# A conformer layer on one core: last keys of four heads in one bank, a VectorE exponential one instruction shorter, half outputs issued beside half scores, and a reordered end

## Chip, cores and metric

The kernel runs on one core of one Trainium2 chip. The metric is the device time of one execution in microseconds (us). The kernel before takes 991.62 us (median of 3 runs, 990.72 to 992.05).

Names used below: PE is TensorE's matrix multiply, PEld its weight load, DVE is VectorE, ACT is ScalarE, POOL is GpSimd. In the views, PT holds exponentials, PS is any bank of PSUM, OTF the attention outputs copied out for their transposes, XN rows normalised by POOL, U the gated input of the convolution, TH a tanh, and HT the hidden layer of a feed-forward.

## The reference

Two sequences of T = 4000 tokens, D = 144 features, H = 4 heads of 36. A feed-forward (half residual), attention, a gated convolution over 5 tokens, a second feed-forward, a layer norm. What matters here is attention, with 2 x 4 x 4000 x 4000 = 128 million exponentials, and the convolution, which couples each token to two neighbours on either side:

```python
scores = jnp.einsum('bhqd,bhkd->bhqk', q, k) * scale
p = _softmax(scores, axis=-1)
att = jnp.einsum('bhqk,bhkd->bhqd', p, v)
...
pad = K // 2                                   # K = 5
hp = jnp.pad(h, ((0, 0), (pad, pad), (0, 0)))
for i in range(K):
    c = c + hp[:, i:i + T, :] * dw[i][None, None, :]
x = x + _silu(c) @ w_pw2
h = _layernorm(x, axis=-1)
h = _silu(h @ w_ff2a) @ w_ff2b
x = x + 0.5 * h
return _layernorm(x, axis=-1)
```

## The kernel before

The program is written by a planner. It keeps an estimated clock for each engine, picks the next piece of work by it, and records instructions. What comes out is a fixed order for each engine with semaphore waits between them; nothing is decided on the chip. So any change of a cost or a rule gives a whole new order.

Queries come in 16 chunks of 500 tokens, keys in 63 tiles of 64 (4000 = 62 x 64 + 32, so the last tile is half padding): 16 x 63 = 1008 tiles. A tile serves 4 heads: in two banks of PSUM, partitions 0 to 63 and 64 to 127 hold two heads each, so one tile is 4 score multiplies of 64 x 64 (one per quadrant of the array), 1000 exponentials on 128 partitions, and 4 output multiplies.

```python
def scores(n, hh, bk, cost):           # half a tile: two heads, one bank, array rows 64*hh
    for p in range(2):
        op("pe", "matmul", PSV[64*p:64*p+64, bk, 0:CH],
           lhsT=KT[64*hh:64*hh+64, p, b, k0:k0+KT_ROWS], rhs=QT[64*hh:64*hh+64, p, q0:q0+CH], ...)

def emit_S(n):                         # a tile for ACT: both halves, all four quadrants
    lo, hi = banks.take_pair()
    scores(n, 0, lo, 0.0525)
    scores(n, 1, hi, 0.0525)

def emit_exp(n, lo, hi):
    op("act", "activation", PT[:, pt, :, :], PSV[:, lo:hi+1, 0:CH], ACT.Exp, scale=ATT_SCALE, ...)

def emit_O(m):                         # outputs of one tile: array rows 64*p
    for hh in range(2):
        for p in range(2):
            op("pe", "matmul", PSV[64*hh:64*hh+DH+1, BX+p, 0:CH],
               lhsT=VA[64*p:64*p+64, blk, hh, 0:DH+1], rhs=PT[64*p:64*p+64, pt, hh, :], ...)
```

Some tiles have their exponential computed on DVE instead, with bit operations and a polynomial. For these the two halves of the scores are issued one at a time, each in its own bank:

```python
def dve_tile(n):
    for hh in range(2):
        bk = yield need("pe", banks, dur=0.21, kind="q")
        scores(n, hh, bk, 0.105)
        ...
        op("dve", "tensor_scalar", PTU[:, z, hh, :], PSV[:, bk, 0:CH], ATT_SCALE*LOG2E*256.0, 127.5*256.0, ...)
    op("dve", "tensor_scalar", mm, zz, 0xFF, 0x6400, op0=bitwise_and, op1=bitwise_or)        # mantissa as f16
    op("dve", "tensor_scalar", zz, zz, 1, 0x7F80, op0=logical_shift_right, op1=bitwise_and)  # exponent
    op("dve", "tensor_scalar", mf, mf, 1.0/256, v - 4.5, op0=mult, op1=add)
    op("dve", "tensor_tensor", mf, mf, mf, op=mult)
    op("dve", "tensor_scalar", mf, mf, E2B, 1.0 - E2B*v*v, op0=mult, op1=add)
    op("dve", "tensor_tensor", PT[:, z], PT[:, z], mf, op=mult)

def due():                             # give the next tile to DVE?
    ...
    return (... and R.free["dve"] < R.free["pe"] + DSLACK and R.free["pe"] > last_dve[0] + DGAP)
```

The end of a chunk (normalising its outputs through transposes, W_o, gate) is `epilogue` and `post1`; convolution, second feed-forward and store are `post2`, which waits for the next chunk's gate because of the two tokens on the right:

```python
def post2(c):
    z = yield need("pe", swp, cond=lambda: c in glu_done and (last or c + 1 in glu_done))
```

The softmax here doesn't subtract the row's maximum and nothing guards it: scores larger than these inputs give would overflow.

Of the kernel before, what the change touches and what calls it, by code (L numbers as in the profile page):

```python
# [12 lines left out]
D = 144  # L13
# [10 lines left out]
CH = 500  # L24
KT_ROWS = 64
# [4 lines left out]
E2A, E2B = 0.7029418, 0.23986403  # L30
# [287 lines left out]
def bass_standalone__conformer_family_zipformer__speech_kernel(  # L318
# [19 lines left out]
    NT = (T + KT_ROWS - 1) // KT_ROWS  # L338
    TP = NT * KT_ROWS

# [25 lines left out]
    BMIN = 1.5  # L366
    DRAIN = 0.6
    LATE = 0.3
    FIRST = 0.3
    DGAP = 4.0  # L370
# [10 lines left out]
    XT = sb("XT", [NXT, 2, CH])  # L381
    XTQ = sb("XTQ", [2, TP])
    TH = sb("TH", [NTH, CH])
    HT = sb("HT", [NHT, 4, CH])
    HT5 = sb("HT5", [NHT, 2 * TB])
    QT = sb("QT", [2, N])
    KT = sb("KT", [2, Bsz, TP])
    VA = sb("VA", [Bsz * NT, 2, 40])
# [6 lines left out]
    SW1 = sb("SW1", [NSW, CH])  # L395
    SW2 = sb("SW2", [NSW, TB])
# [66 lines left out]
    op("pool", "memset", NHALF[:, :], -0.5, w=["NHALF"])  # L463
    op("act", "activation", DUM[:, :], NHALF[:, 0:1], ACT.Silu, bias=0.0, scale=1.0, r=["NHALF"], w=["DUM"], cost=1.6)
# [10 lines left out]
    op("dve", "memset", KT[:, :, :, T:TP], 0.0, w=["KTZ"])  # L475
    op("dve", "memset", XTQ[:, :, T:TP], 0.0, w=["XTQZ"])
    op("dve", "memset", VA[:, :, :, DH:DH + 1], 1.0, w=["VA1a"], cost=0.5)
    tail_rows = T - (NT - 1) * KT_ROWS
    if tail_rows < KT_ROWS:
        for half in range(2):  # L480
            for b in range(Bsz):
                r0 = 64 * half + tail_rows
                op("dve", "memset", VA[r0:64 * half + 64, b * NT + NT - 1, :, DH:DH + 1], 0.0, r=["VA1a"],
                   w=["VA1"], cost=0.2)
# [30 lines left out]
    def copy(dst, src, r, w, n, rate=1.0):  # L515
        if flex() == "act":
            op("act", "activation", dst, src, ACT.Copy, bias=0.0, scale=1.0, r=r, w=w, cost=c_act(n))
        else:
            op("dve", "tensor_copy", dst, src, r=r, w=w, cost=c_dve(n, rate))

    def setup_dw():
# [18 lines left out]
        for i in range(KCONV):  # L540
            op("dve", "tensor_scalar", DG[:, i, :], IDENT[:, :], DWT[:, 0, i:i + 1], None, op0=ALU.mult,
               r=["DWT", "ID"], w=["DG"], cost=0.2)
        for o in range(3):
# [16 lines left out]
    def transp(src, rk, dst, wk, n):  # L560
        bk = yield need("pe", banks, dur=0.11 * n)
        ps = PSH[0:HD, bk, 0:256 * n].rearrange("p (k i n) -> p k i n", k=2, i=n)
        for k in range(2):
            for i in range(n):
                op("pe", "transpose", ps[:, k, i, 0:TB], src[:, i, k * HD:(k + 1) * HD], IDENT[0:TB, 0:TB],
                   r=[rk, "ID"], w=[("ps", bk)], cost=0.055, kind="f")
        yield need("dve", hold=True)
        copy(dst.rearrange("p k (i n) -> p k i n", i=n), ps[:, :, :, 0:TB], [("ps", bk)], wk, 2 * n * TB, 2.0)
        banks.give(bk)

    def ln(c, bs):
        n, b0 = len(bs), bs[0]
        u = yield need("dve", xnp)
        for j in range(n):
            op("dve", "bn_stats", ST[0:TB, u, j, :], X[0:TB, c * NB + b0 + j, :], r=[("X", c, b0 + j)],
               w=[("ST", u, j)], cost=0.21)
        yield need("dve")
        for j in range(n):
            op("dve", "bn_aggr", MV[0:TB, u, j, :], ST[0:TB, u, j, :], r=[("ST", u, j)], w=[("MV", u)], cost=0.08)
        calm = mode["front"] or mode["tail"]  # L580
# [8 lines left out]
        if not calm:  # L589
            op("pool", "tensor_scalar", RS[0:TB, u, 2, 0:n], MV[0:TB, u, 0:n, 0], -1.0, None, op0=ALU.mult,  # L590
               r=[("MV", u)], w=[("NM", u)], cost=0.3)
            for j in range(n):
                op("pool", "tensor_scalar", XN[0:TB, u, j, :], X[0:TB, c * NB + b0 + j, :], RS[0:TB, u, 2, j:j + 1],
                   RS[0:TB, u, 0, j:j + 1], op0=ALU.add, op1=ALU.mult,
                   r=[("X", c, b0 + j), ("NM", u), ("RS", u)], w=[("XN", u)], cost=XN_COST)
        else:
            yield need("dve")
            for j in range(n):
# [5 lines left out]
    XN_COST = 0.5  # L604
    POW_COST = 1.1

    def ln_tr(c, s, bs):
        u = yield from ln(c, bs)
        yield from transp(XN[0:TB, u, 0:len(bs), :], ("XN", u), XT[0:HD, s, :, bs[0] * TB:(bs[-1] + 1) * TB],
                          [("XT", s, i) for i in bs], len(bs))  # L610
        xnp.give(u)
# [11 lines left out]
    def residual(c, g, mm, scale, rk):  # L623
# [3 lines left out]
        for i in range(2):  # L627
# [8 lines left out]
           cost=c_dve(2 * D))  # L636
        banks.give(bk)

    def mm2(W0, s, m0, m1, bk, rows, wk):
        for k in range(2):  # L640
            op("pe", "matmul", PSV[0:rows, bk, 0:CH], lhsT=W0[0:HD, k, m0:m1], rhs=XT[0:HD, s, k, :], start=k == 0,
# [7 lines left out]
    def ff_tile(s, h, m, WA, WE, nm, silu):  # L649
# [4 lines left out]
        if m < 4:  # L654
            mm2(WA, s, m * 128, m * 128 + 128, bk, 128, [(nm, "a", 0)])
            n, dst = CH, HT[:, h, m, :]
        else:
            for k in range(2):
                for g in range(2):
                    op("pe", "matmul", PSV[:, bk, 0:2 * TB], lhsT=WE[0:HD, k, 64 - 64 * g:192 - 64 * g],  # L660
                       rhs=XT[0:HD, s, k, g * 2 * TB:(g + 1) * 2 * TB], start=k == 0 and g == 0, stop=k == 1 and g == 1,
                       r=[("XT", s, 2 * g), ("XT", s, 2 * g + 1), (nm, "a", 1), (nm, "a", 2), (nm, "a", 3)], w=[("ps", bk)], cost=c_pe(2 * TB),
                       kind="f")
            n, dst = 2 * TB, HT5[:, h, :]
# [13 lines left out]
    def ff(c, s, WA, WE, WB, nm, silu, then):  # L678
        h = yield need("pe", htp)
        kids = S.spawn(ff_tile(s, h, m, WA, WE, nm, silu) for m in range(5))  # L680
# [6 lines left out]
        def terms(i):  # L687
            return [(HT[:, h, m, i * TB:(i + 1) * TB], WB[:, m, :]) for m in range(4)] + [
                (HT5[:, h, (i % 2) * TB:(i % 2 + 1) * TB], WB[:, 4 + i // 2, :])]

        def half(g):
            yield from residual(c, g, terms, 0.5 if silu else 0.25, [("HT", h)] + [(nm, "b", j) for j in range(5)])
# [15 lines left out]
    def proj(dst, Wt, nm, c, p):  # L708
# [8 lines left out]
        copy(dst, PSV[:, bk, 0:CH], [("ps", bk)], [(nm + "T", c)] + [("SAVE", i) for i in range(NQ) if over], CH)  # L717
        banks.give(bk)
# [3 lines left out]

    def vproj(c, t0, t1):
# [3 lines left out]
        rk = ["WQKV", "XTQZ"] + [("XTQ", cc, i) for cc in range(CPB) for i in range(NB)  # L727
# [9 lines left out]
        copy(VA[:, b * NT + t0:b * NT + t1, :, 0:DH],  # L737
# [19 lines left out]
    def pre2(c):  # L757
# [9 lines left out]
        t0, t1 = (tiles_by(cc - 1) if cc else 0), tiles_by(cc)  # L767
        vs = []
# [57 lines left out]

    def post1(c, a):
# [20 lines left out]
        kids = S.spawn((glu(c, s2), glu_left(c, s2)))  # L848
        yield need("pool", kids=kids, cond=lambda: cc == 0 or c - 1 in glu_done)
        xtp.give(s2)  # L850
        u, up = c % NU, (c - 1) % NU
        if cc == 0:
            op("pool", "memset", U1[:, u, 2:4, 0:1], 0.0, w=[("UL", u)], cost=0.1)
            op("pool", "memset", U2[0:LP, u, 0:1], 0.0, w=[("UL", u)], cost=0.1)
        else:
            op("pool", "tensor_copy", U1[:, u, 2:4, 0:1], U1[:, up, 2:4, TB:TB + 1], r=[("U", up)], w=[("UL", u)],
               cost=0.25)
            op("pool", "tensor_copy", U1[:, up, 0:2, TB + 1:TB + 2], U1[:, u, 0:2, 1:2], r=[("U", u)],
               w=[("UR", up)], cost=0.25)
            op("pool", "tensor_copy", U2[0:LP, u, 0:1], U2[0:LP, up, TB:TB + 1], r=[("V", up)], w=[("UL", u)],  # L860
               cost=0.25)
            op("pool", "tensor_copy", U2[0:LP, up, TB + 1:TB + 2], U2[0:LP, u, 1:2], r=[("V", u)], w=[("UR", up)],
               cost=0.25)
        if cc == CPB - 1:
            op("pool", "memset", U1[:, u, 0:2, TB + 1:TB + 2], 0.0, w=[("UR", u)], cost=0.1)
            op("pool", "memset", U2[0:LP, u, TB + 1:TB + 2], 0.0, w=[("UR", u)], cost=0.1)
        glu_done.add(c)

    def conv(c, z, silu):
# [18 lines left out]
        yield from conv_act(z, bk, None if silu else t, ML, SW1[:, z, :], "SW", CH)  # L888
# [16 lines left out]
    def conv_left(c, z, silu):  # L905
# [8 lines left out]
        yield from conv_act(z, bk, None if silu else t, LP, SW2[0:LP, z, :], "SX", TB)  # L914

    def post2(c):
        cc = c % CPB
        last = cc == CPB - 1
        z = yield need("pe", swp, cond=lambda: c in glu_done and (last or c + 1 in glu_done))
# [380 lines left out]
```

## Time and profile before

| | before |
|---|---|
| time, median | 991.62 us |
| span of the profiled execution | 988.6 us |
| front, until the first exponential | 25.2 us |
| body, first to last exponential | 920.7 us |
| tail, from there to the end | 42.7 us |
| tiles on ACT / on DVE | 899 / 109 |

The busy time of the body and of the tail (columns: length, then busy us and instructions of PE, PEld, DVE, ACT, POOL; granted clock, DMA share, GB/s):

```profile
25.24:945.93 920.69, 865.75 (x10935) 369.31 (x10933) 792.07 (x2058) 900.19 (x1114) 281.42 (x487) 1.00 0.01 4
945.93:988.60 42.67, 34.23 (x441) 29.38 (x441) 25.00 (x106) 12.07 (x24) 9.12 (x18) 0.93 0.04 11
```

ACT works 900.2 of the body's 920.7 us. DVE's groups of the exponential by shape (busy us, mean ns | idle before):

```profile
L167 DVE TENSOR_TENSOR PT<-PT 128x1000 bf16<-128x1000 bf16 x109 | 74.2, 685 | 0.9
L167 DVE TENSOR_TENSOR PT<-PT 128x1000 f16<-128x1000 f16 x109 | 73.1, 678 | 0.9
```

Who is on the chain that ended last, and how long exponentials waited for scores (us, times, longest):

```profile
ACT 56%; PE 29%; DVE 11%; POOL 3%; issue 1%; POOLq 0%; DVEq 0%
```

```profile
ACT PT L167 <- PE PS L167: 13.8, 23, 1.8
```

The mean duration of a group on ACT includes overlap with its neighbours. For sums I therefore took from the trace's ACT records of the body, for each instruction, by how much its end passes the end before it ("occupied"), and the gap before it ("idle"). Before: 899 exponentials occupy 811.9 us (0.903 each), 141 tanh of 500 elements 68.6, the rest 19.7; sum 900.2 occupied, 20.5 idle.

A part of this idle time comes in single stops, which the prediction did not look at. PE waits for a tile that POOL makes, and ACT then waits for PE. One of them:

```profile
142.05 0.63 PE L167 MATMUL PS<-IDENT,XN 125*72 125x125 bf16 x8 [1.98 <-POOL XN L167]
```

```profile
142.75:146.16 3.41, 3.41 (x31) 1.22 (x24) 0.71 (x2) 2.30 (x3) 2.74 (x6) 0.50 0.00 0
```

PE stood still for 1.98 us, and 0.70 us after it goes on its granted clock falls to 0.50 for 3.41 us (third number from the end); ACT is busy for only 2.30 us of these. The body before has two such pairs (at 142 and 695 us) and one more stop of over 1 us for POOL (at 749 us). Together 5.1 of the 20.5 us of idle lie at them.

### The profile page before, as it was taken

To read this page: it belongs to the slowest core of one execution; us is meant where nothing else is said; L and a number is where in the kernel's file an instruction comes from. 1 tells how busy PE (TensorE), PEld (TensorE's weight loads), DVE (VectorE), ACT (ScalarE), POOL (GpSimd) and SP (SyncE) were. 2 spreads that over 40 slices of the span, in tenths; PEclk is the share of its full clock that TensorE was granted. 3 is DMA by queue.
4 is the path that set the end of the run, shared out by engine and by line. 5 is a ranking of instruction groups with operands and counts; after the bars stand their busy time and mean duration, and the time that the engine had idled before them with its cause. 6 is when DMAs were issued, how large, how long until landed. Compare 5 with 4: busy or idle time off the path is not lost.

```text
span 988.6 us, 27456 instructions
## 1 busy us (share of the span) xinstructions
PE 923.5 (93%) x11672; PEld 418.0 (42%) x11672; DVE 836.8 (85%) x2260; ACT 924.2 (93%) x1159; POOL 298.5 (30%) x525
## 2 busy tenths in 40 slices
PE   9999989999999999999999999999899999999997
PEld 7443424343443434444444344343344333434365
DVE  7888777999699798977879898899899997985965
ACT  4898989999999999999999999999999999999943
POOL 3221032132442225313714132235112522433212
PEclk9999999999999999999999999999999999999999
DMA  4000000000000000000000000000000000000000
GB/s 123 14 1 2 1 2 2 2 2 1 3 1 2 2 2 8 1 2 14 1 2 7 2 8 1 7 8 2 1 7 2 7 2 7 8 2 7 7 8 13
DMA packets 7422, 7.36 MB, mean 7 GB/s; under 512 B 2349, under 2 KB 7300, under 8 KB 7300
## 3 DMA queue, kind: packets, MB, share of 16 engines
q1 hardware_dynamic: 6144, 5.14, 1.8%
q8 instruction: 91, 1.49, 0.7%
q10 hardware_dynamic: 1156, 0.47, 0.2%
q14 instruction: 31, 0.25, 0.1%
HBM read 3.31 MB, written 2.30 MB: 6 GB/s over the span
## 4 chain that ended last, share of the span: by engine, by line
ACT 56%; PE 29%; DVE 11%; POOL 3%; issue 1%; POOLq 0%; DVEq 0%
ACT PT L167 50%; PE PS L167 29%; ACT TH L167 6%; DVE PT L167 5%; POOL XN L167 2%; POOL RS L167 1%; DVE ST L167 1%; DVE HT L167 1%; DVE XT L167 1%; DVE X L167 1%; DVE OTF L167 0%; DVE AN L167 0%; DVE MV L167 0%; DVE QT L167 0%; ACT HT L167 0%
## 5 line engine op out<-in xcount | busy, mean ns | idle before, releaser
L167 ACT ACTIVATE PT<-PS 128x1000 bf16<-128x1000 f32 x899 | 839.0, 1063 | 15.7 <-PE PS L167 13.8
L167 PE MATMUL PS<-QT,KT 64*64 64x500 bf16 x4032 | 419.1, 385 | 34.5 <-ACT PT L167 26.4
L167 PE MATMUL PS<-PT,VA 64*37 64x500 bf16 x4032 | 364.0, 377 | 6.4 <-ACT PT L167 2.9
L167 PEld LDWEIGHTS PS<-QT,KT 64*64 64x64 bf16 x4032 | 125.7, 104 | 236.1 <-ACT PT L167 170.2
L167 POOL TENSOR_SCALAR RS<-MV 125x4 f32<-125x4 f32 x116 | 39.0, 336 | 472.6 <-DVE MV L167 467.8
L167 DVE TENSOR_SCALAR PT<-PT 128x1000 uint16<-128x1000 uint16 (+1 forms) x436 | 177.1, 419 | 5.0
L167 PEld LDWEIGHTS PS<-PT,VA 64*37 64x37 bf16 x4032 | 115.8, 95 | 125.9 <-issue 36.8
L167 DVE TENSOR_SCALAR PT<-PS 128x500 uint16<-128x500 f32 x218 | 145.9, 670 | 16.4 <-PE PS L167 15.3
L167 POOL TENSOR_SCALAR XN<-X,RS 125x144 bf16<-125x144 bf16 x232 | 146.2, 642 | 6.0
L167 DVE TENSOR_TENSOR PT<-PT 128x1000 f16<-128x1000 f16 (+1 forms) x218 | 145.6, 681 | 1.8
L167 POOL TENSOR_TENSOR RS<-RS,NHALF 125x4 f32<-125x4 f32 (+1 forms) x102 | 99.4, 976 | 128.3 <-DVE RS L167 123.2
L167 ACT ACTIVATE TH<-PS 128x500 bf16<-128x500 f32 (+2 forms) x205 | 111.8, 570 | 3.2 <-PE PS L167 2.9
L167 DVE SCALAR_TENSOR_TENSOR HT<-TH,PS 128x500 bf16<-128x500 bf16 (+1 forms) x145 | 87.0, 616 | 27.2 <-ACT TH L167 26.3
L167 DVE SCALAR_TENSOR_TENSOR X<-PS,X 125x288 bf16<-125x288 f32 x128 | 57.1, 453 | 31.3 <-PE PS L167 29.8
L167 DVE BATCH_NORM_STATS2 ST<-X 125x6 f32<-125x144 bf16 x320 | 75.4, 295 | 2.4 <-DMA X<-in_x_dram 2.1
L167 PE MATMUL PS<-XT,WA 72*128 72x500 bf16 x256 | 72.6, 379 | 3.0 <-DVE HT L167 2.6
L167 PE MATMUL PS<-WB,HT 128*125 128x144 bf16 x640 | 61.2, 234 | 0.3
L167 PEld LDWEIGHTS PS<-WB,HT 128*125 128x125 bf16 x640 | 47.4, 137 | 26.0 <-issue 16.3
L167 PE MATMUL PS<-IDENT,XN 125*72 125x125 bf16 x512 | 42.8, 221 | 6.7 <-POOL XN L167 5.0
L167 DVE COPY XT<-PS 72x1000 bf16<-72x1000 bf16 (+1 forms) x65 | 40.2, 620 | 8.3 <-PE PS L167 7.9
L167 PEld LDWEIGHTS PS<-IDENT,XN 125*72 125x72 bf16 x512 | 31.4, 112 | 26.7 <-issue 11.4
L167 POOL COPY U<-U 128x2 bf16<-128x2 bf16 (+1 forms) x56 | 12.6, 256 | 79.2 <-DVE U L167 79.2
(78 smaller groups left out, 627.8 us busy)
## 6 DMA issues: line engine op xcount, KB each, us to landing
X<-in_x_dram SPq DMA_DIRECT2D x16, 140.6 KB
out_dram<-XN SPq DMA_DIRECT2D x13, 140.6 KB
out_dram<-XN SPq DMA_DIRECT2D x6, 70.3 KB
WA<-in_w_ff1a_dram ACTq DMA_DIRECT2D x1, 144.0 KB
WB<-in_w_ff1b_dram ACTq DMA_DIRECT2D x1, 144.0 KB, 2.7
WA<-in_w_ff2a_dram SPq DMA_DIRECT2D x1, 144.0 KB
WB<-in_w_ff2b_dram SPq DMA_DIRECT2D x1, 144.0 KB
WQKV<-in_w_qkv_dram ACTq DMA_DIRECT2D x1, 121.5 KB
```

The source lines that it names most:

```text
L167: ins = getattr(eng, o.name)(*o.a, **o.k)
```

## The change

The intent is to take exponentials off ACT, in four parts. (1) The last 32 keys: 32 keys of four heads fill 128 partitions of one bank, so the last tile of a chunk costs 500 exponentials in place of 1000. (2) DVE's chain loses one instruction: the exponent is no longer cut out; the polynomial is added to the integer form, as a mixed uint16 and f16 addition. (3) A half score of a DVE tile is issued beside half an output of another tile, on the other rows of the array. (4) At the end, chunk 15 goes first and carries the last two tokens of chunk 14, so chunk 14's convolution does not wait for it; the output copy of chunk 15 is split over DVE and ACT. `BMIN`, a limit on finished chunks whose later stages lag behind, goes from 1.5 to 2.0.

```diff
-    BMIN = 1.5
+    BMIN = 2.0
 def emit_S(n):
+    if t == NF:                                    # (1) last 32 keys: one bank
+        for p in range(2):
+            op("pe", "matmul", PSV[64*p:64*p+64, bk, 0:CH], lhsT=KL[:, b, p, :], rhs=QT[:, p, c*CH:(c+1)*CH], ...)
+        return bk, None
 def emit_exp(n, lo, hi):
+    if hi is None:
+        op("act", "activation", PT[:, pt, 0, :], PSV[:, lo, 0:CH], ACT.Exp, ...)
+        return
 def dve_tile(n):
-        scores(n, hh, bk, 0.105)
+        m = partner(1 - hh)                            # (3) an output whose input is ready
+        scores(n, hh, bk, 0.105 if m is None else 0.0525)
+        if m is not None:
+            emit_O(m, (1 - hh,))
...
-    op("dve", "tensor_scalar", zz, zz, 1, 0x7F80, op0=logical_shift_right, op1=bitwise_and)      # (2)
-    op("dve", "tensor_scalar", mf, mf, 1.0/256, v - 4.5, op0=mult, op1=add)
+    op("dve", "tensor_scalar", mf, mf, sc/256, (off - 4)*sc, op0=mult, op1=add)
     op("dve", "tensor_tensor", mf, mf, mf, op=mult)
-    op("dve", "tensor_scalar", mf, mf, E2B, 1.0 - E2B*v*v, op0=mult, op1=add)
-    op("dve", "tensor_tensor", PT[:, z], PT[:, z], mf, op=mult)
+    op("dve", "tensor_tensor", zz, zz, mf, op=add)
+    op("dve", "tensor_scalar", zz, zz, 256*(E2[0] - 1) - (off*sc)**2, 0.5, op0=add, op1=mult)
...
 def epilogue(c, part):                                # (4)
+    elif c == NCH - 1:
+        op("dve", "tensor_copy", OTF[:, 0, :], ps[:, 0, :], ...)
+        op("act", "activation", OTF[:, 1, :], ps[:, 1, :], ACT.Copy, ...)
 def post2(c):
-    cond=lambda: c in glu_done and (last or c + 1 in glu_done)
+    cond=lambda: c in glu_done and (last or c == NCH - 2 or c + 1 in glu_done)
+    e = c == NCH - 1                                   # two more columns in conv, residuals, norms
```

The cuts leave out how the two extra tokens pass through each stage, and how half-issued outputs are counted. The diff holds three more changes that are in none of the four parts: the planner now counts rows normalised by POOL as ready 0.5 us after their instruction ends, in place of 0.1 (`XN_LAT`); the convolution's border copies on POOL are planned as a thread of their own (`halo`); and the four output multiplies of a tile are issued by array rows (`for p ... for hh`) and no longer by columns.

## The prediction

> **What bounds the kernel now.** I read the page first (busy shares, slices), then the busy time by stretch, then the groups by shape, then the chain of waits, and last the timeline of the end. Three engines look full on the page:
>
> ```profile
> PE 923.5 (93%) x11672; PEld 418.0 (42%) x11672; DVE 836.8 (85%) x2260; ACT 924.2 (93%) x1159; POOL 298.5 (30%) x525
> ```
>
> A mean over the span hides which one is full where the time is spent. The table by stretch (columns: busy us and instruction count of each engine, granted clock, DMA share, GB/s) shows it:
>
> ```profile
> 0.00:25.00 25.00, 23.28 (x296) 19.25 (x298) 19.48 (x96) 11.93 (x22) 7.99 (x20) 1.00 0.45 123
> 200.00:300.00 100.00, 97.04 (x1275) 43.49 (x1274) 85.92 (x228) 99.18 (x121) 36.56 (x71) 1.00 0.01 2
> 700.00:800.00 100.00, 92.59 (x1175) 39.25 (x1175) 94.56 (x228) 98.94 (x121) 25.37 (x42) 1.00 0.02 5
> 950.00:989.00 39.00, 31.52 (x413) 26.95 (x411) 23.48 (x104) 11.81 (x23) 9.12 (x18) 0.94 0.05 13
> ```
>
> ACT (the fourth pair) is at 99% from 200 to 900 us; DVE is below it, and PE's 92 to 97% is pipelined, overlapping time. The chain of waits says the same: 50% of the span is ACT writing PT (the exponentials). So there are three parts: a front of 25 us, a body from 25.2 us to 945.9 us paced by ACT, and a tail of 42.7 us (988.6 - 945.9) in which ACT is nearly idle and one dependency chain sets the end. The change leaves the front's ACT order as it is (the first 123 ACT instructions of the two streams are the same), so I work on body and tail only.
>
> What one ACT instruction costs in the body has to be read from the chain, because the mean of a group (1063 ns) includes overlap with its neighbours:
>
> ```profile
> 924.28 14.35 ACT PT L167 x16
> 938.62 0.48 ACT TH L167
> 939.10 2.69 ACT PT L167 x3
> ...
> 945.03 0.91 ACT PT L167
> 945.93 0.04 issue
> 945.98 0.42 PE PS L167 x4
> 946.40 0.02 issue
> 946.42 1.21 DVE OTF L167
> ```
>
> 14.35/16 = 0.897 us for a full exponential (1000 elements), 0.48 us for a tanh of 500. Check of the whole body: 899 exponentials x 0.897 = 806.4; 141 tanh of 500 x 0.48 = 67.7; 27 tanh of 250 x 0.27 = 7.3; 29 small tanh x 0.17 = 4.9; copies (15 x 0.48 and two small) 7.5; sum 893.8 of 920.7 us. The other 26.9 us are ACT's idle time (20.5 by the same table over the body, over half of it before 150 us) and small gaps.
>
> The tail, in the timeline of PE:
>
> ```profile
> 945.98 0.39 PE L167 MATMUL PS<-PT,VA 64*37 64x500 bf16 x4 [0.42 <-ACT PT L167]
> 947.68 2.43 PE L167 MATMUL PS<-IDENT 128*128 128x128 bf16 x26 [1.31 <-DVE OTF L167]
> 949.91 1.16 PE L167 MATMUL PS<-IDF,OTF 128*125 128x128 f32 x4
> 950.86 1.51 PE L167 MATMUL PS<-WB,HT 128*125 128x144 bf16 x15
> 952.21 0.65 PE L167 MATMUL PS<-IDF,OTF 128*125 128x128 f32 x4
> ```
>
> The 26 filler multiplies write into the bank that the OTF copy reads, so they wait for the copy and then run in front of the transposes that need it: 2.2 us lost.
>
> **What the Trainium skill says.** "ScalarE: Activation LUTs", section "What ACT_TABLE_LOAD costs": 186 ns + 0.833 ns per element, back-to-back instructions overlapping by about 93 ns. That gives 0.926 us for 1000 and 0.51 us for 500; the trace has 0.897 and 0.48, so a half-width exponential costs 0.48, more than half of a full one. "VectorE: DVE Perf Modes", section "The perf-mode tier table": 16-bit tensor_scalar in SBUF runs 4x, tensor_tensor 2x, a PSUM source at most 2x; the trace agrees (1000 elements: 415 to 424 ns and 678 to 685 ns; 500 from PSUM 670 ns). Its section "What auto-detection actually checks" makes the mode a matter of 16-bit size, not of type, so the new uint16 + f16 addition should keep 2x; no instruction of this trace mixes the two, so it is unproven here. "TensorEngine Tiling (Array Packing)", section "Key Properties": tiles of the array work independently, and a change of tiling mode drains the engine. The trace agrees on the first: 8 quadrant multiplies last 0.61 us, 4 last 0.39, so four more cost 0.22, one full pass.
>
> **The change part by part.** The counts are of the instruction streams of the two built programs.
>
> (1) Last keys. Of 1008 key tiles (16 chunks x 63), 16 have only 32 real keys, and half the partitions of their 1000-wide exponential were padding. Now the 32 keys of all four heads share the 128 partitions of one bank: 16 exponentials of 500. PE gains nothing: two 500-column multiplies on 64 columns each in place of four quadrant ones, both about 0.21 us.
>
> (2) Shorter VectorE chain. A tile on VectorE took 2 reads from PSUM, 4 tensor_scalar and 2 tensor_tensor; by the means of their groups 2 x 670 + 4 x 420 + 2 x 681 ns = 4.38 us. Now one tensor_scalar less: 3.96 us. With that room the order gives VectorE 123 tiles in place of 109. VectorE's busy sum for this: 109 x 4.38 = 477 before, 123 x 3.96 = 487 after: 10 us more, in a shorter span: about 850/964 = 88%. The saving is spent on taking work from ACT.
>
> (3) So ACT's full exponentials go from 899 to 869. The sum for ACT's body: -30 x 0.897 = -26.9; +16 x 0.48 = +7.7; six tanh of 500 and one of 250 leave the body (a feed-forward of a late chunk now falls into the tail, partly from the higher backlog limit): -6 x 0.48 - 0.27 = -3.2. **Together -22.4 us**, body 920.7 to about 898. With 98% of ACT's time busy there, I take this one to one and leave the 26.9 us of idle and gaps unchanged.
>
> (4) Half outputs beside half scores. 204 of 246 half scores get a partner, but only 30 output tiles are split over two partners; 144 have one half riding and the other alone, which in full passes saves nothing. Saved: 30 x 0.21 = 6.3 us; the 14 more VectorE tiles cost 14 x 0.21 = 2.9, and the engine changes between kinds of work 35 times more. For PE a wash; PE is not the bound, so 0 us on the path. It makes room, no more.
>
> (5) Tail. Chunk 15 goes first and carries two tokens of chunk 14, whose convolution no longer needs chunk 15. In the stream: the OTF copy is split over DVE and ACT (1.21 to about 0.67: -0.5); four real multiplies stand where the 26 fillers stood, and don't wait for OTF (-2.2); between the two transposes stand 4 multiplies of 0.21 in place of 15 of 0.06 (-0.6); the 31 fillers before the convolution give way to 15 real multiplies (-0.8). Against it: a feed-forward of an earlier chunk, with five Silu (2.3 us) and the table load (1.28 us), now lies on ACT ahead of the copies that the chain needs (+0.7, my guess), and from the convolution to the last multiply the stream holds 17.2 us by the rates above against 15.7 (+1.5: extra two-column multiplies, two convolutions one after the other with fillers between). **Sum about -1.9 us**: tail 42.7 to 40.8. The order at the end stays: chunk 15's feed-forward, then chunk 14's, then its normalisation and store. So the dependence that is removed is only partly used.
>
> Sum: 991.6 - 22.4 - 1.9 = **967 us**, 2.5% less.
>
> **The rivals.** (a) VectorE becomes the bound. For it: it reached 94.6% in 700 to 800 us, single stretches of 10 us are above 97%. Against: in that very stretch ACT was still at 98.9%, and a tile now costs 0.4 us less. If ACT's idle grew by half its 20.5 us: 977. (b) The mixed addition falls to one element per cycle: 1000/0.96 ns in place of 500/0.96, +0.5 us x 123 = 64 us of VectorE, 95% busy; ACT would then wait often: 985 to 1000. (c) PE, its order fixed at build time, stalls where a half output is not ready when the order expects it, and the scores behind it come late: a few us, 970 to 972. (d) PE profits more than counted, because a half output alone overlaps with the next half pass on the other rows, and removes some of the 13.8 us that exponentials wait for PE: 960 to 963.
>
> **Range and chances.** ACT's count is certain; what isn't is idle time in the body (-4 to +8) and the tail (-3 to +3). That gives 960 to 975 for 8 in 10. The 2% line is at 971.8, 4.8 us above my value: 0.80 for faster by over 2%, 0.18 within, 0.02 slower, the last for (b) with more.
>
> **What would show it.** Right: the last exponential ends near 923 us, 869 full ones at 0.897 and 16 halves near 0.48, ACT at 98 to 99% from 200 us on; the mixed addition near 680 ns, no group of DVE at 1.1 us; DVE near 88%; the tail 39 to 43 us, with the transposes of OTF about 1 us after the last output. Wrong: ACT idle well above 21 us in the body (a, c), an addition at 1.1 us (b), exponentials slower than 0.897, or a tail that grows because chunk 13's leftovers delay chunk 15.

## More of the kernel before

All executions used here are fast, with a mean granted TensorE clock between 0.988 and 1.00. Time and clock go together: of the 21 executions of the kernel before that were timed beside the experiments, the eight at 0.990 took 992.05 to 992.78 us, the seven at 0.993 took 989.87 to 990.61, and the only one at 0.997 took 987.92.

## The result, and the profile after

The kernel after takes **968.89 us** (median of 4, 968.71 to 969.11) against 991.73 (median of 4) for before. The ratio is 0.9772 (95% interval 0.9755 to 0.9788). A ratio here is always the mean time of one kernel's fast runs over that of the other's of the same rounds, so not quite the ratio of the quoted medians. The profiled span is 967.1 us, 21.5 less than before. About 3 us of the difference go with the clock: the one execution of the kernel before at the clock of the kernel after, 0.997, took 987.92 us where the mean of its 21 is 991.08 (an estimate, from that single execution).

```profile
PE 911.4 (94%) x11539; PEld 411.2 (43%) x11539; DVE 849.0 (88%) x2271; ACT 907.9 (94%) x1147; POOL 295.0 (31%) x521
```

The same table for one stretch of the body, for the body and for the tail:

```profile
200.00:300.00 100.00, 96.08 (x1244) 41.89 (x1238) 91.07 (x221) 95.89 (x119) 32.98 (x60) 1.00 0.01 2
```

```profile
25.24:925.88 900.64, 854.62 (x10839) 365.73 (x10835) 797.51 (x2042) 879.92 (x1093) 276.50 (x482) 1.00 0.01 4
925.88:967.10 41.22, 33.23 (x408) 26.26 (x404) 31.48 (x134) 15.97 (x33) 10.51 (x18) 0.93 0.06 15
```

The body is 20.0 us shorter, the tail 1.5, the front is the same. ACT's busy time in the body fell by 20.3 us, its idle time did not move (20.5 and 20.7 us by my sum). In 200 to 300 us ACT is now at 95.9%, so the equal sum hides a change of place. The body after has no stretch at half clock, and one stop of PE for POOL of over 1 us (1.54 us, at 604 us) with 0.7 us of ACT's idle at it. So the stops gave back 4.4 us, and idle elsewhere grew by 4.6 (15.4 to 20.0).

ACT's and DVE's groups by shape:

```profile
L168 ACT ACTIVATE PT<-PS 128x1000 bf16<-128x1000 f32 x869 | 811.4, 1050 | 15.0 <-PE PS L168 13.5
...
L168 ACT ACTIVATE PT<-PS 128x500 bf16<-128x500 f32 x16 | 10.1, 630 | 0.1
```

```profile
L168 DVE TENSOR_TENSOR PT<-PT 128x1000 uint16<-128x1000 uint16 x123 | 83.9, 685 | 1.1
L168 DVE TENSOR_TENSOR PT<-PT 128x1000 f16<-128x1000 f16 x123 | 83.7, 683 | 1.3
```

The mixed addition (the uint16 group) takes 685 ns, as the f16 multiply beside it takes 683. The chain has changed more than the sums have:

```profile
ACT 48%; PE 35%; DVE 14%; POOL 2%; issue 1%; POOLq 0%; DVEq 0%
```

Before, 56% of the chain was ACT; now 48%, with PE and DVE taking the difference. More often than before, the piece that ended last came through a score or a DVE tile. That was the first sign that "ACT alone sets the pace" is not the whole story.

The end, in PE's timeline (start us, us, tiles, count):

```profile
926.25 0.41 PE L168 MATMUL PS<-PT,VL 64*101 64x500 bf16 x2
926.60 1.02 PE L168 MATMUL PS<-XT,WA 72*128 72x500 bf16 x4
927.45 0.68 PE L168 MATMUL PS<-IDF,OTF 128*125 128x128 f32 x4
...
928.82 0.60 PE L168 MATMUL PS<-IDF,OTF 128*125 128x128 f32 x4
```

Four real multiplies stand where the 26 fillers stood, and the transposes of OTF start 1.20 us after the last outputs start (927.45 - 926.25), where before it was 3.93 us (949.91 - 945.98). Part of that is clock: before, PE was at half clock from 948.30 to 951.71 us. Later in the tail, ACT's timeline (the value in brackets is idle time before, and who ended it):

```profile
951.06 2.31 ACT L168 ACTIVATE HT<-PS 128x502 bf16<-128x502 f32 x5 [0.69 <-PE PS L168]
...
955.35 1.54 ACT L168 ACTIVATE HT<-PS 128x500 bf16<-128x500 f32 x3 [1.53 <-PE PS L168]
```

HT of 502 columns is chunk 15's last feed-forward (500 and the two riders); HT of 500 after it is chunk 14's, which therefore ends last, with its normalisation and store behind it.

### The profile page after: what moved, and what is told of

It reads as the page before. It is cut to its first block, busy times and chain, and to the rows that moved or that the text cites. A ratio compares the mean times of both kernels' runs of the same rounds, so it can differ in the third digit from the quotient of the medians.

```text
span 967.1 us, 27192 instructions
## 1 busy us (share of the span) xinstructions
PE 911.4 (94%) x11539; PEld 411.2 (43%) x11539; DVE 849.0 (88%) x2271; ACT 907.9 (94%) x1147; POOL 295.0 (31%) x521
## 4 chain that ended last, share of the span: by engine, by line
ACT 48%; PE 35%; DVE 14%; POOL 2%; issue 1%; POOLq 0%; DVEq 0%
ACT PT L168 42%; PE PS L168 35%; DVE PT L168 8%; ACT TH L168 5%; DVE ST L168 1%; POOL XN L168 1%; DVE X L168 1%; POOL RS L168 1%; DVE HT L168 1%; DVE XT L168 1%; ACT HT L168 0%; DVE OTF L168 0%; DVE MV L168 0%; DVE XN L168 0%; DVE AN L168 0%
## 5 line engine op out<-in xcount | busy, mean ns | idle before, releaser
L168 ACT ACTIVATE PT<-PS 128x1000 bf16<-128x1000 f32 x885 | 819.3, 1043 | 15.1 <-PE PS L168 13.5
L168 PE MATMUL PS<-PT,VA 64*37 64x500 bf16 x3968 | 375.7, 376 | 7.0 <-ACT PT L168 3.8
L168 DVE TENSOR_SCALAR PT<-PS 128x500 uint16<-128x500 f32 x246 | 164.5, 670 | 19.7 <-PE PS L168 18.8
L168 DVE TENSOR_TENSOR PT<-PT 128x1000 f16<-128x1000 f16 (+1 forms) x246 | 166.9, 684 | 2.4
L168 DVE TENSOR_SCALAR PT<-PT 128x1000 uint16<-128x1000 uint16 (+1 forms) x369 | 152.0, 423 | 3.0
L168 POOL TENSOR_SCALAR XN<-X,RS 125x144 bf16<-125x144 bf16 x228 | 137.4, 615 | 5.9
L168 POOL TENSOR_TENSOR RS<-RS,NHALF 125x4 f32<-125x4 f32 (+2 forms) x103 | 98.7, 960 | 122.7 <-DVE RS L168 117.6
L168 DVE SCALAR_TENSOR_TENSOR HT<-TH,PS 128x500 bf16<-128x500 bf16 (+1 forms) x140 | 83.8, 615 | 15.9 <-ACT TH L168 15.4
L168 PE MATMUL PS<-XT,WA 72*128 72x500 bf16 (+1 forms) x256 | 72.9, 379 | 2.6 <-DVE HT L168 1.2
L168 PEld LDWEIGHTS PS<-WB,HT 128*125 128x125 bf16 x645 | 47.1, 135 | 26.2 <-issue 15.6
L168 PE MATMUL PS<-IDENT,XN 125*72 125x125 bf16 (+1 forms) x514 | 42.9, 221 | 3.9 <-POOL XN L168 2.0
L168 PEld LDWEIGHTS PS<-IDENT,XN 125*72 125x72 bf16 (+1 forms) x514 | 31.5, 112 | 24.3 <-issue 9.8
```

What stands on the lines that cost most here:

```text
L168: ins = getattr(eng, o.name)(*o.a, **o.k)
```

## The experiments

The number was close, but it rested on two claims that the profile after makes doubtful: that pairing half outputs with half scores is worth nothing on the path because PE is not the bound, and that DVE's added work lies beside ACT. Theory A in the expectations is the prediction's own account; the other letters are its rivals. Each kernel was timed against the kernel before in the same rounds; after's own ratio is 0.9772, taken in other rounds, so differences between a variant and after are differences of two ratios, times 991 us. They are not corrected for the clock. All twelve gave the reference's result.

A word on method: e1 to e8 are planned anew, so each has its own order. e9 and e10 keep after's order on every engine and add work inside it.

| run | tiles on DVE | ratio | against after, us | body, us | ACT occupied / idle, us | tail, us | of idle, at stops, us |
|---|---|---|---|---|---|---|---|
| before | 109 | 1 |  | 920.7 | 900.2 / 20.5 | 42.7 | 5.1 |
| after | 123 | 0.9772 |  | 900.6 | 879.9 / 20.7 | 41.2 | 0.7 |
| e1 | 120 | 0.9893 | +12.0 | 912.2 | 882.0 / 30.2 | 41.2 | 5.6 |
| e2 | 117 | 0.9788 | +1.6 | 904.4 | 884.9 / 19.6 | 38.7 | 0.0 |
| e3 | 109 | 0.9857 | +8.4 | 913.3 | 893.2 / 20.1 | 36.6 | 0.0 |
| e4 | 122 | 0.9817 | +4.5 | 907.1 | 886.8 / 20.3 | 37.5 | 0.7 |
| e5 | 121 | 0.9813 | +4.1 | 907.6 | 881.5 / 26.2 | 37.2 | 3.5 |
| e6 | 116 | 0.9957 | +18.3 | 917.3 | 894.1 / 23.2 | 41.1 | 3.2 |
| e7 | 116 | 0.9995 | +22.1 | 921.3 | 895.7 / 25.7 | 40.3 | 8.4 |
| e8 | 123 | 0.9849 | +7.6 | 903.2 | 878.8 / 24.3 | 49.5 | 4.3 |
| e9 | 123 | 0.9837 | +6.4 | 906.5 | 883.2 / 23.3 | 41.2 | 0.8 |
| e10 | 123 | 1.0197 | +42.1 | 941.0 | 893.9 / 47.2 | 41.9 | 4.0 |
| e11 | 131 | 0.9732 | -4.0 | 898.3 | 873.6 / 24.8 | 37.6 | 7.3 |
| e12 | 132 | 0.9730 | -4.2 | 899.2 | 874.2 / 25.0 | 35.8 | 3.0 |

The front, not in the table, varies from 24.7 to 26.9 us. The last column is ACT's idle time within 1 us before and 5.5 us after each stop of PE of over 1 us that POOL ended, and around two stretches at half clock that no such stop precedes (e8 at 55 us, e10 at 944). Of the 15 stretches at half clock in the bodies of all traces, 13 follow such a stop; seven stops of 1.03 to 1.64 us are followed by none. Where these stops fall changes with the order, so they blur every comparison of two orders.

One more measure: the score and output multiplies of the trace that start within 60 ns of each other (up to four) were counted as one pass of the array. The kernel before needs 2181 passes, after 2120, and "half-filled" below means a pass with two multiplies.

### e1_no_pair: no half output beside a half score

```diff
 def partner(p):
+    return None
```

> The changed kernel without the pairing of half outputs with half scores; all else as changed; the scheduler then gives VectorE 120 tiles in place of 123. Theory A (my prediction: ACT's count alone sets the body, PE is a wash): three exponentials more on ACT, 3 x 0.90 = +2.7 us, about 971.6 us, ACT idle in the body still near 20.7 us. Rival B (the pairing makes room on PE that the path needs): 975 us or more, with ACT idle in the body of 25 us or more, waiting for PE.

Measured 980.45 us (980.12 to 980.78), ratio 0.9893 (0.9878 to 0.9908). The body is 11.6 us longer than after's. Three more exponentials on ACT are 2.3 us of that (788.0 - 785.7 occupied; 2.1 in the sum of all ACT work); 9.5 us are ACT idle, 4.9 of them at stops for POOL. This is the line of waits for ACT, of e1:

```profile
ACT PT L168 <- PE PS L168: 23.3, 32, 2.4
```

After has 13.5 us there (its group line above). What pairing does is seen in PE's timeline. After, around 277 us:

```profile
277.41 0.40 PE L168 MATMUL PS<-QT,KT 64*64 64x500 bf16 x2
277.41 0.39 PE L168 MATMUL PS<-PT,VA 64*37 64x500 bf16 x2
```

and e1, around 309 us:

```profile
308.72 0.37 PE L168 MATMUL PS<-QT,KT 64*64 64x500 bf16 x2
308.96 0.40 PE L168 MATMUL PS<-PT,VA 64*37 64x500 bf16 x4
```

In after, two score multiplies and two output multiplies start in the same hundredth of a microsecond: one pass for both. In e1 the half score has 0.24 us to itself before the four outputs start. Over the kernel, e1 has 2177 passes, 374 of them half-filled; after has 2120 and 264. The 57 passes x 0.21 us are 12 us of PE time. That this is the size of the loss is chance: e9 below shows 0.07 us of body for each added pass, so 57 passes are some 4 us (an estimate), which fits the 4.6 us by which idle grew away from the stops. The prediction had saved only 30 passes. Theory A's 971.6 is off by 9 us for this order.

### e5_no_pair_alt: the same with another order

```diff
-    DSLACK = 0.6
+    DSLACK = 0.4
-    DGAP = 4.0
+    DGAP = 3.5
 def partner(p):
+    return None
```

> Again no pairing, but with two scheduler settings changed (least gap between VectorE tiles 3.5 in place of 4.0, slack 0.4 in place of 0.6), so that another order comes out (121 tiles). It separates the pairing from the luck of one order. Theory C (without pairing PE runs some 57 passes of 0.21 us more and ACT waits for it): 975 us or more, ACT idle in the body 26 us or more, 2165 quadrant passes or more. Rival (the +11.6 us of the first run without pairing were one unlucky order): 972 us or less.

Measured 972.25 us (970.53 to 972.82), ratio 0.9813 (0.9790 to 0.9836). Also without pairing, but 8 us faster than e1. The two expectations are split: the total is at the rival's bound, the idle at Theory C's. Body +7.0 us over after, 5.5 of it ACT idle, 2.8 of that at one stop of PE for POOL of 2.74 us; 2161 passes, 41 more than after; the tail is 4.0 us shorter. So taking pairing away costs the body 7.0 to 11.6 us in these two orders, but 2.8 to 4.9 of that are stops, which no run ties to pairing. What is left, 4.2 to 6.7 us, is idle elsewhere (2.6 and 4.6) and exponentials (1.6 and 2.1). The order alone moves the total by several us. That is the error bar of every single variant that is planned anew.

### e2_long_chain: the old six-operation chain on DVE

```diff
-        zz, zz + mf (uint16 + f16), then (zz + k) * 0.5
+        zz = (zz >> 1) & 0x7F80; mf = mf*E2B + k; PT = PT * mf        # one instruction more
```

> The changed kernel with the longer VectorE chain of before (4 tensor_scalar and 2 tensor_tensor per tile); the scheduler then takes 117 tiles. Theory A: six exponentials more on ACT, 6 x 0.90 = +5.4 us, about 974.3 us, ACT idle unchanged near 21 us, VectorE at about 90% (117 x 4.38 = 512 us of tiles against 487). Rival (VectorE becomes the bound with the long chain): above 978 us with ACT idle above 26 us.

Measured 970.09 us (969.95 to 970.21), ratio 0.9788 (0.9774 to 0.9803). The longer chain gets 117 tiles in place of 123; six exponentials more on ACT, body +3.8 us, of the size of 6 x 0.90 = 5.4 less 1.1 of idle. But the tail is 2.6 us shorter, so little is left in the total. The expectation, 974.3, was 4.2 us too slow, most of it because it held the tail constant. Its rival, DVE as the bound with the long chain, is out for this order: idle did not grow.

### e3_cap_109: everything new, but DVE gets no more tiles than before

```diff
-        if n >= NIT or not DVE_EXP or ...
+        if n >= NIT or stats["dve"] >= 0.1062 * n + 2 or not DVE_EXP or ...
```

> The changed kernel with VectorE's tiles held to 109, spread evenly, as many as before. Theory A: 14 exponentials go back to ACT, 14 x 0.90 = +12.6 us, about 981.5 us, ACT idle near 20 us. Rival (the gain comes from PE room or other waits, not from the count): below 976 us.

Measured 976.94 us (976.52 to 977.23), ratio 0.9857 (0.9843 to 0.9872). Its body:

```profile
25.24:938.50 913.26, 867.60 (x10893) 368.19 (x10891) 764.65 (x1969) 893.16 (x1113) 274.53 (x496) 1.00 0.01 4
```

The body is 12.6 us longer than after's, and 14 x 0.90 = 12.6. Idle is the same (20.1 and 20.7). This is the best test of the prediction's main term, that a tile moved from DVE to ACT costs its exponential, one to one; it is one order, planned anew, without any stop for POOL. The total lies between the two expectations, only 8.4 us slower, because the tail is 4.7 us shorter.

### e4_full_last: the last tile padded and two banks wide, as before

```diff
-    NF = T // KT_ROWS;  NT = NF + 1          # last tile apart, in one bank
+    NT = NF = (T + KT_ROWS - 1) // KT_ROWS   # with the zero padding and its memsets back
```

> The changed kernel with the last 32 keys as before: a padded 1000-wide tile in two banks in place of one bank of 500. 886 full exponentials in place of 869 full and 16 half: 17 x 0.904 - 16 x 0.498 = +7.4 us. Theory A: about 976.3 us. Rival (the one-bank form costs PE drains at the change of array mode, which this takes away): 972 to 974 us.

Measured 971.82 us (971.56 to 975.21), ratio 0.9817 (0.9795 to 0.9840). Full exponentials 886 in place of 869, no halves: 17 x 0.904 - 8.0 = +7.4 by the sum; ACT occupied +6.9 (its exponentials 800.7 against 785.7 and 8.0), body +6.5. The term holds in the body; the tail gave 3.8 back, so the total came out at the rival's 972 us. Idle did not fall (20.3), so the rival's reason, drains of PE in the body, is not seen; it is not excluded either.

### e6_pair_only and e7_short_only: one part alone

e6 is built from the kernel after, with the other three parts and `BMIN` set back; the three further changes named above and the priority of chunk 15 at the end stay in it. e7 is the kernel before with only the shorter chain.

```diff
 # e6, what differs from before, in the main (the record has its diff against after)
+        m = partner(1 - hh)
+        scores(n, hh, bk, 0.105 if m is None else 0.0525)
+        if m is not None: emit_O(m, (1 - hh,))
 # e7, against before
+        the five-operation chain in dve_tile, nothing else
```

> Pairing alone: the changed kernel with the long VectorE chain, the padded last tile, no tokens riding, no split copy and the old backlog limit. The scheduler finds 116 tiles. Theory C (PE's passes are the second bound, so pairing pays by itself): 7 exponentials off ACT, -6.3 us, and a little idle: 981 to 985 us beside 990.6. Rival (my prediction: pairing is a wash by itself, VectorE's room is what is needed): 989 us or more.

> The shorter VectorE chain alone, put into the kernel before; 116 tiles. My prediction's sum: 7 exponentials off ACT, 7 x 0.90 = -6.3 us: 984.3 us, ACT idle unchanged at 20.5 us. Theory C: more VectorE tiles mean more half-filled PE passes, so without pairing ACT's idle grows to 25 us or more and half or more of the gain is lost: 987 us or more.

e6: 985.70 us (985.43 to 987.79), ratio 0.9957 (0.9933 to 0.9980). e7: 989.62 us (988.43 to 992.12), ratio 0.9995 (0.9969 to 1.0021). Both have 892 exponentials on ACT in place of 899, so 6.3 us less by the sum. e6 keeps 3.4 of it in the body. e7 keeps none: occupied falls by 4.5 and idle rises by 5.2 (20.5 to 25.7). I read that at first as PE's extra passes (2204, 23 more than before) coming back as waits of ACT. The trace doesn't bear this out. e7 has four stops for POOL, three of them followed by 3.41 us at half clock; the longest:

```profile
144.39 0.63 PE L167 MATMUL PS<-IDENT,XN 125*72 125x125 bf16 x8 [3.14 <-POOL XN L167]
```

They hold 8.4 us of its idle, where before has 5.1: 3.3 of the 5.2. Away from the stops idle grew by 1.8 us in e7, and by 4.6 in e6, which has pairing and some 30 passes fewer than before. So these two runs don't show that passes decide. The mean clock of e7's runs (0.991) was also lower than that of the kernel before beside it (0.993). The shares of the parts don't add up: 0.4% and 0.05% alone, while undoing pairing in the whole costs 0.4 to 1.2%.

### e8_no_ride: chunk 14's two tokens wait for chunk 15 again

```diff
-        e = c == NCH - 1
+        e = False
-        cond=lambda: c in glu_done and (last or c == NCH - 2 or c + 1 in glu_done)
+        cond=lambda: c in glu_done and (last or c + 1 in glu_done)
```

> The changed kernel with chunk 14's last two tokens not riding with chunk 15 (chunk 14's convolution waits for chunk 15 again); priorities and the split copy stay; 123 tiles. My prediction gives riding little: body as in the changed kernel (900.6 us), tail 41 to 43 us: 969 to 971 us. Rival (with chunk 15's priority the dependence holds chunk 14 back to the end): tail 45 us or more, 974 us or more.

Measured 975.40 us (975.37 to 980.30, 5 runs), ratio 0.9849 (0.9824 to 0.9874). The profiled execution was the longest of the five (span 978.5, the others 973.5 to 973.8); it has two stretches at half clock, at 55 and 608 us, so in the body. Its tail is 49.5 us against 41.2. So the riding is worth about 8 us in the tail by the profile, and 6.5 (medians) to 7.6 us (ratio) in the total, far more than the net of 1.5 suggests: without the riding, the end of this order is slower (49.5) than that of the kernel before (42.7).

### e9_pe_extra: more PE work, same order

Every second DVE tile issues its first half score twice. The result is the same, and so is the order on every engine.

```diff
         scores(n, hh, bk, 0.105 if m is None else 0.0525)
+        if hh == 0 and stats["dve"] % 2:
+            scores(n, hh, bk, 0.0)
```

> The changed kernel, the same instruction order on every engine, with one addition: in every second VectorE tile the first half score is issued twice (62 times two quadrant multiplies, the second overwriting the first with the same values): 62 x 0.21 = 13 us of PE, about what the runs without pairing had more. Theory C (PE is the second bound of the body, ACT pays for its passes): ACT idle in the body rises by 7 us or more, to 28 us or more, and the time to 976 us or more. Rival (PE has slack; those runs were slower for their order alone): 971 us or less, idle under 23 us.

Measured 974.76 us (974.26 to 976.41), ratio 0.9837 (0.9821 to 0.9853). 62 half scores at 0.21 us a pass are 13.0 us of PE (the trace counts 84 passes more, because some that were full are now split); the body grew by 5.9 us, 45% of the 13.0. That is 0.07 us for each of the 84 passes. Between the two expectations: PE is neither the bound nor free. The order of the instructions on DVE, ACT and POOL is after's one by one, and the stops are the same, so this is free of the blur above. The chain of e9:

```profile
PE 45%; ACT 43%; DVE 9%; POOL 2%; issue 1%; POOLq 0%; DVEq 0%
```

PE's share is up from 35%. ACT's visible idle grew by only 2.6 us; the other 3.3 show as longer occupied time. I read these as small waits hidden in the overlap of one ACT instruction with the next (from one exponential's start to the next it is 0.884 us at best, and one occupies 0.904 in the mean).

### e10_dve_extra: more DVE work, same order

The first bit operation of each of the 123 tiles is done twice, with the same result; the order is after's. So each of these tiles is also ready 0.42 us later on its own account.

```diff
+    op("dve", "tensor_scalar", mm, zz, 0xFF, 0x6400, op0=bitwise_and, op1=bitwise_or, ...)   # again
```

> The changed kernel, the same order on every engine, with the first bit operation of each of the 123 VectorE tiles done twice with the same result: 123 x 0.42 = 52 us more of VectorE, about 94% busy in place of 88%. If VectorE has the slack that my prediction assumed: at most +3 us, 972 us or less, ACT idle under 23 us. If VectorE's chain is on the path (the planned order leaves it no reserve): 977 us or more, with ACT or PE waiting for PT from VectorE.

Measured 1009.97 us (1008.93 to 1014.00), ratio 1.0197 (1.0172 to 1.0222). The group of bit operations is 123 instructions longer at 0.42 us: 52 us of DVE. The total grew by 42 us, 80% of it. Body and chain of e10:

```profile
25.20:966.20 941.00, 864.67 (x10835) 364.52 (x10832) 844.61 (x2160) 893.82 (x1093) 274.49 (x482) 1.00 0.01 4
```

```profile
DVE 57%; PE 31%; ACT 8%; POOL 2%; issue 1%; POOLq 0%; DVEq 0%
```

DVE's share of the chain went from 14% to 57%, ACT's from 48% to 8%, although DVE's busy share in the body is just 844.61/941.00 = 90%. How the time gets from DVE to ACT is in the waits. PE's weight loads waiting for a DVE tile, e10 and then after:

```profile
PEld PS L168 <- DVE PT L168: 93.7, 208, 1.6
```

```profile
PEld PS L168 <- DVE PT L168: 49.9, 153, 0.8
```

By what they are for, these are weight loads of outputs, which wait for a late DVE tile (41.1 us, after 14.8), and of scores, whose bank DVE has yet to empty (28.1 us, after 13.4). In PE's fixed order both stand in front of the scores that ACT needs next. PE waits for DVE, and ACT for PE (31.7 us of exponentials waiting for scores, where after has 13.5). Of 52 us only 10 found room beside a busy share of 88%. Not all of the 42 are DVE's: 4.0 of the 47.2 us of idle lie at two stretches at half clock, where after has 0.7.

### e11_tuned_a and e12_tuned_b: other settings of the planner

If idle time, order and tail trade against each other, the planner's settings should be worth a little. I swept them with the planner's own clock as a guide and ran two.

```diff
 # e11                          # e12
-    DSLACK = 0.6                -    DSLACK = 0.6
+    DSLACK = 1.0                +    DSLACK = 0.4
-    AHEAD = 0.64; OFREE = 3; FIRST = 0.3       (both)
+    AHEAD = 0.55; OFREE = 2; FIRST = 0.2       (both)
-    HALF = 5; DRAIN = 0.6
+    HALF = 4; DRAIN = 0.4
```

> The changed kernel with six scheduler settings changed and nothing else; VectorE then gets 131 tiles. If the body is ACT's count with idle unchanged: 8 x 0.90 = -7.2 us, about 961.7 us. If PE and VectorE are too full to carry 8 more tiles: idle grows and it stays above 966 us.

> The changed kernel with four scheduler settings changed; VectorE gets 132 tiles. ACT's count: 9 x 0.90 = -8.1 us, about 960.8 us. If PE and VectorE are too full: above 966 us.

e11: 964.43 us (963.88 to 964.98), ratio 0.9732 (0.9716 to 0.9748). e12: 963.88 us (963.54 to 966.26), ratio 0.9730 (0.9712 to 0.9747). Both beat the kernel before by 2.7%, and after by about 0.4% by their ratios (after was not run in the same rounds). Both lie between their two expectations. Of e12's 5.2 us of span, the body gives 1.5 and the tail 5.4, while the front is 1.7 us longer. Nine fewer exponentials are worth 7.5 us of occupied time, but other work on ACT takes 1.8 us back and idle 4.3. This is no proof that PE and DVE are too full: e11's idle rose by 4.1 us, and 7.3 us of it lie at two stops of PE for POOL (3.25 and 2.71 us); away from them it is 17.4 us, less than after's 20.0, with 131 tiles on DVE. Its tail shows what after's does not do (ACT's timeline of e12):

```profile
943.13 2.46 ACT L168 ACTIVATE HT<-PS 128x500 bf16<-128x500 f32 x5 [1.11 <-PE PS L168]
...
950.20 2.31 ACT L168 ACTIVATE HT<-PS 128x502 bf16<-128x502 f32 x5 [0.69 <-PE PS L168]
```

Chunk 14's feed-forward (500 columns) now comes 7 us before chunk 15's (502 columns), which ends last. The tail is 35.8 us. e2, e3, e4, e5 and e11 end in the same way, with 36.6 to 38.7.

## Why the prediction was right in its number, and where not

**The three parts and the count of exponentials: right.** Body predicted -22.4 us, measured -20.0; tail -1.9, measured -1.5. By ACT's occupied time: full exponentials -26.9 predicted, -26.2 measured (811.9 to 785.7); half ones +7.7 against +8.0; tanh -3.2 against -2.6; small rises in the rest make up 0.5 and idle 0.2. e3 shows the main term in one order (14 tiles, 12.6 us), e4 the half exponentials (+6.5 for 7.4; one takes 0.50 us, where the prediction had the 0.48 of a tanh). Of the signs it named, one did not come: ACT is at 95.9% and 97.6% from 200 to 400 us, not at 98 to 99%.

**Idle unchanged: right as a sum, by luck.** It took ACT's idle as constant because ACT was 98% busy. It stayed constant (20.5 and 20.7 us) because two things met that the prediction didn't have: idle at the stops for POOL and the half clock that follows fell by 4.4 us, and idle elsewhere rose by 4.6. Why the stops became fewer is not shown; the planner's new figure for POOL (`XN_LAT`) is one candidate, the mere change of order another. That 14 more tiles with their scores by halves raise the idle elsewhere, and pairing lowers it (e1 and e5, away from the stops: 4.6 and 2.6 us more without it), is likely and not shown. So the 2 us between prediction and result say less for the mechanism than they seem to.

**Step (4), pairing as "a wash, 0 us on the path": wrong.** Two things failed. The step's count, "144 have one half riding and the other alone, which in full passes saves nothing", gave 30 passes; against e1 they fell by 57, against e5 by 41. Why, stays open. It is not simply that a half left alone meets another half: e1, without pairing, has 221 passes that mix scores and outputs, nearly as many as after with 237 (before, with its other order of outputs, has 152). And "PE is not the bound, so 0 us on the path" was wrong as an inference: e9 shows 45% of added PE time on the path with the order fixed; and without pairing the body is 4.2 to 6.7 us longer in two orders even with the stops taken out. The rival (d), PE profiting more than counted, had the direction right; its consequence, a time of 960 to 963, did not come. The rival (c), PE held up by a half that is not ready, was not isolated: weight loads wait 49.9 us for DVE tiles, before 45.6.

**Step (2), room on DVE: right in its durations, wrong in its reading.** 3.98 us for a tile and 88% busy came out as predicted, and the mixed addition kept its speed (685 ns), so rival (b) is out. But most of the 12% that is left is not room. With the order fixed, 52 us more on DVE cost 42 (e10). Rival (a) asked whether DVE becomes the bound; the answer is that PE, ACT and DVE are bound to each other by the fixed order, and through the stops POOL too, so that the busiest is not the only one on the path. The prediction read a busy share below 100% as room; the wait of PE for DVE's tiles, and of ACT for PE, is what it left out.

**Step (5), the tail: net right, terms not.** The transposes came 1.2 us after the last outputs, as expected. One sum is wrong as written: 4 multiplies of 0.21 in place of 15 of 0.06 us save 0.1, not 0.6; the 15 took 1.51 us in the trace, in part at half clock, and the two groups of transposes now start 1.37 us apart in place of 2.30. The riding is worth about 8 us (e8), and the order in which a left-over feed-forward of an earlier chunk delays chunk 14's to after chunk 15's gives part of that back. The tails fall into two groups by this: where chunk 15's feed-forward comes last (e2, e3, e4, e5, e11, e12), 35.8 to 38.7 us; where chunk 14's comes after it, as in after, e1, e9 and e10, 41.2 to 41.9. The prediction saw that "the dependence that is removed is only partly used", but not that it was worth that much.

**What stays open.** Undoing a part makes a new order, and e1 and e5 differ by 8 us for the same rule. So the values of single parts (pairing 4 to 12 us in total, stops included; shorter chain 1.6, last tile 4.5) are of that accuracy; only e9 and e10, with the order kept, are free of it. Part of this scatter is the stops for POOL with the half clock after them; no run changed them alone. That finishing chunk 14 first shortens the tail is read from the two groups above; no run changed this alone.

## What to carry to other kernels

In a kernel whose engines run in fixed orders, an engine's busy share doesn't tell what more work on it will cost: add a known amount inside the unchanged order and measure, as in e9 and e10. Count what a change does to the engine that feeds the bound one, in the units in which that engine works (here passes of the array), before calling it 0 on the path. When a planner writes the order, one build of a variant is one draw: two draws of the same rule tell how far a few microseconds can be trusted. Before the difference of two orders is put down to the part that was changed, look in both traces for single long stops and for the granted clock: here they held up to 8.4 us of a body.

## What the Trainium skill lacked or had wrong

- "TensorEngine Tiling (Array Packing)", section "Key Properties", says that tiles execute in parallel and that a change of mode drains the engine; no page has what the drain costs. The trace agrees with the first (277.41 us above: four multiplies in the same 10 ns). From the last multiply of one quadrant pass to the next pass it is 214 ns (median of some 1500 in the trace of after), to a multiply of 72 x 128 (all columns) 327 ns (median of 88): some 0.11 us for the change, with whatever waits are in it.
- "VectorE: DVE Perf Modes", section "What auto-detection actually checks", has nothing to correct: its rule, by size, held for a case for which it has no example, an addition of uint16 and f16 (685 ns for 1000 elements; a multiply of f16 alone 683).
- "Perfetto Trace Analysis", section "Identifying the Most-Contended Engine", goes by the highest occupancy for ScalarE and VectorE. Here ACT has 94% and DVE 88%, and still 52 us added to DVE cost 42 us, for the orders are fixed. No page says how to tell from a trace what added work on an engine will cost.
